# Transform tables as two 16-bit whole numbers per value, both parts written by ScalarE

## The chip, the cores and the metric

The kernel runs as one program on one core of a Trainium2 chip. The metric is the device time of one execution, in microseconds (us). The core has a matrix engine (TensorE, PE in the profile, with its weight loads as PEld), VectorE (DVE), ScalarE (ACT), GpSimd (POOL) and a queue engine that issues transfers (SyncE, SP).

## The reference

Three stages follow each other:

```python
X = np.fft.fft(x, axis=1); X = np.fft.fft(X, axis=2); x = X.real     # x: 8 x 3072 x 256
logits = x @ w_gate; e = argmax(logits); p = softmax(logits)[e]      # 8 experts, 768 tokens each at most
out[i] = p * (relu(x[i] @ w1[e]) @ w2[e])      # the first tokens of each expert only, 0 for the rest
h = out @ w_in; y = maximum(0.01 * h, h) @ w_out                     # 256 -> 2048 -> 256
```

Only the first 768 tokens of each expert are kept, in the order of the sequence. The kernel transforms just as many batches as it takes to fill the experts, and a branch at the end covers inputs for which these do not do.

## The kernel before, in words

All matrix work is done in pairs: a value is held as a high part and a low part (`split`, L190: ScalarE copies the value into a tile of the matrix format, which rounds it; VectorE subtracts that from the value), and a product takes three matmuls (`mm3`, L194, the matmuls of L199 to L201).

The transform along the sequence is a product with cosine and sine tables. `shape_consts` (L46) computes them on the host, 128 x 6918 values. `load_table` (L293) brings them in three parts j, each in two halves of 128 x 1153: a transfer into a staging tile `tst`, then one step that splits it into `th` and `tl`. SP's transfers run in the order of the code: the first block of x (`xj`), two halves of tables, the next block of x, two halves, the third block, two halves, then small constants.

Before the matmuls, `fold_steps` (L329) folds each block of x on VectorE: two large sums and differences (`fe`, `xj`), then smaller ones down to `raw`. Three blocks make a batch. `fsplit_j` (L409) splits `raw` into `fh` and `fl`. `s1_first` (L512) multiplies these by the tables for batch 0, block by block, into eight banks. `s1_ev_odd` and `s1_ev_even` (L454, L467) take them out to `pch`, `pcl`, `psh`, `psl`. `build_gate` (L251) makes the movable matrix of the second transform with the gate's columns, `smov` for one of the rows that need an own treatment, `special` (L581) the stationary side of these, `spec`. Then `s2_steps` (L622) runs the transform along the channels: its first matmul (L643, `psu<-smov,spec`) needs both. The first three batches (0, 1 and half of 2) go through this, with the folds of the next batch and the routing of the last (`route`, L709) strewn in between. Then the tokens are gathered and go through the experts (`moe_static`, L1257) and through the dense layers at the end.

On all engines but SP the order of instructions comes from a list scheduler, which works from its own estimates of durations when the program is built. A change of one step's cost or engine can therefore move other instructions.

Of the kernel before, what the change touches and what calls it, by code (L numbers as in the profile page):

```python
# [8 lines left out]
F32 = mybir.dt.float32  # L9
F32R = mybir.dt.float32r  # L10
BF16 = mybir.dt.bfloat16
I32 = mybir.dt.int32
ALU = mybir.AluOpType
ACTF = mybir.ActivationFunctionType
AX = mybir.AxisListType
# [5 lines left out]
P = 128  # L21
# [14 lines left out]
TJ = 2306  # L36
T_OFF = {"A": (0, 384), "B": (768, 384), "C": (1152, 386), "D": (1538, 384), "E": (1922, 384)}
T_W = 3 * TJ


def s_rows():

    return np.concatenate([np.arange(0, 384, 2), np.arange(1, 384, 2)]).reshape(3, P)


def shape_consts():  # L46
    w = 2 * np.pi / S
    n = np.arange(384)
    nc_ = np.arange(386)
    parts = []  # L50
    for s in s_rows().astype(np.float64):
        z = s == 0
        u2 = np.where(z, 384, 768 - s)
        s3 = np.where(z, 384, s)
        tc_ = np.cos(w * np.outer(s, 4 * nc_))
        tc_[:, 385] = 0.0
        te = np.sin(w * np.outer(s, 4 * n))
        te[z] = 0.0
        parts += [np.cos(w * np.outer(s, 4 * n + 1)), np.cos(w * np.outer(u2, 4 * n + 1)),
                  np.cos(w * np.outer(s, 4 * n + 2)), tc_, np.sin(w * np.outer(s3, 4 * n + 2)), te]  # L60
    c = {"tab": np.concatenate(parts, 1).astype(np.float32)}
    assert c["tab"].shape == (P, T_W)
    alt = np.zeros((1, 386), np.float32)
    alt[0, :385] = (-1.0) ** np.arange(385)
    c["altn"] = alt
    d = np.arange(P, dtype=np.float64)
    l = np.arange(D, dtype=np.float64)
    cd = np.cos(2 * np.pi / D * np.outer(d, l))
    sd = np.sin(2 * np.pi / D * np.outer(d, l))
    cd[0] = 1.0  # L70
    sd[0] = 0.0
    c["mcs"] = np.stack([cd, sd, -sd], 1).astype(np.float32)
    altl = (-1.0) ** l - 1.0
    lt = np.concatenate([cd.T.reshape(2, P, P), sd.T.reshape(2, P, P),
                         np.repeat(altl.reshape(2, P, 1), 96, axis=2)], 2)
    c["mcsT"] = np.ascontiguousarray(
        np.concatenate([lt[:, :, :256], lt[:, :, 256:]], 2).transpose(1, 0, 2)).astype(np.float32)

    def spec(nb):
        m = np.zeros((96, nb, D), np.float32)  # L80
        k = np.zeros((96, nb, 2), np.float32)
        for b in range(nb):
            for h in range(2):
                r = h * nb + b
                m[r, b] = altl
                m[32 + r, b] = altl
                k[r, b, 0] = k[32 + r, b, 0] = 1.0
                k[64 + r, b, 1] = 1.0
        return m, k

    c["sm3"], c["sk3"] = spec(NSTAT)
    c["sm1"], c["sk1"] = spec(1)
    p = np.arange(P)
    tri = np.stack([(p[:, None] < p[None]), (p[:, None] > p[None]), np.ones((P, P))], 1)
    c["tri"] = tri.astype(np.float32)
    rid = np.full((P, NCH), 1536.0 + 3 + P, np.float32)
    tok = np.full((P, NCH), 1536.0, np.float32)
    inval = np.zeros((P, NCH), np.float32)
    for i in range(3):
        for r in range(4):  # L100
            k = 4 * (128 * i + p) + r
            tok[:, 4 * i + r] = k
            rid[:, 4 * i + r] = P + k
            mcol = 13 + 4 * (2 - i) + 3 - r
            tok[:, mcol] = S - k
            rid[:, mcol] = P + 1536 + 4 * (128 * i + p) + 3 - r
    inval[1:, 12] = 100.0
    inval[0, 24] = 100.0
    inval[:, 25] = 100.0
    rt = np.stack([rid, tok], 1)  # L110
    c["rt"], c["inval"] = np.stack([rt + S * b for b in range(NSTAT)], 1).astype(np.float32), inval
    c["iota"] = np.tile(p, (P, 1)).astype(np.float32)
    c["w8"] = np.tile(8.0 - np.arange(8, dtype=np.float32), (P, 1))
    keep = np.ones((P, E, NG + 1), np.float32)
    keep[:, :, 0] = 0.0
    c["keep"] = keep
    return c
# [26 lines left out]
class Kern:  # L144
# [39 lines left out]
    def tt(self, o, x, y, op):  # L184
        self.nc.vector.tensor_tensor(out=o, in0=x, in1=y, op=op)  # L185
# [4 lines left out]
    def split(self, hi, lo, src):  # L190
        self.act(hi, src)
        self.tt(lo, src, hi, ALU.subtract)

# [57 lines left out]
    def build_gate(self, tmp, nb):  # L251
# [24 lines left out]
        for b in range(nb):  # L276
            t0 = tmp.tile([96, E], F32, name="smt0", tag="smt0")
            V.tensor_scalar(out=t0, in0=wh.bitcast(F32), scalar1=sk[:, b, 0:1], scalar2=None, op0=ALU.mult)
            t1 = tmp.tile([96, E], F32, name="smt1", tag="smt1")
            V.tensor_scalar(out=t1, in0=wl.bitcast(F32), scalar1=sk[:, b, 1:2], scalar2=None, op0=ALU.mult)  # L280
            self.tt(mv[:, b, D:], t0, t1, ALU.add)

# [6 lines left out]
    def open_tables(self):  # L289
        self.th = self.big.tile([P, T_W + 13 * 96], F32R, name="th", tag="bhi")  # L290
        self.tl = self.big.tile([P, T_W], F32R, name="tl", tag="blo")

    def load_table(self, pt, j):  # L293

        nc, a = self.nc, self.a
        st = []
        h = TJ // 2
        for i in range(2):
            t = pt.tile([P, h], F32, name="tst", tag=("pch", "pcl", "psh", "psl")[2 * (j % 2) + i])
            o = j * TJ + i * h  # L300
            nc.sync.dma_start(out=t, in_=a["tab"][:, o:o + h])
            st.append((1.3, lambda t=t, o=o: self.split(self.th[:, o:o + h], self.tl[:, o:o + h], t)))
        return st

    def tab(self, n, j, half=0):
# [23 lines left out]
    def fold_steps(self, b):  # L329
# [7 lines left out]
        tt = self.tt  # L337
        A, M = ALU.add, ALU.subtract

# [114 lines left out]
    def s1_ev_odd(self, fn, pa, pb):  # L454
# [5 lines left out]
        t3 = self.yp.tile([P, n], F32, name="t3", tag="ev", bufs=3)  # L460
        self.tt(t1, pa[:, :n], tb, ALU.add)
        x, y = (pa[:, :n], tb) if fn == "c" else (tb, pa[:, :n])
# [88 lines left out]
    def special_fold(self):  # L551
# [15 lines left out]
        tt(raw[0:1, 3, 0], ce[0:1, :, 0, 0], c7, A)  # L567
        st = self.th[:, T_W:].rearrange("p (k r) -> p k r", k=13)
        nc.gpsimd.memset(st.bitcast(F32), 0.0)
# [139 lines left out]
    def route(self, b, L, n):  # L709
# [9 lines left out]
        def t2(name, dt=F32):  # L719
            return rp.tile([P, NCH], dt, name=name, tag=name)[:, :n]  # L720
# [41 lines left out]
        def two():  # L762
# [31 lines left out]
            V.tensor_scalar(out=bad, in0=bad, scalar1=BIG, scalar2=float(E * self.capp), op0=ALU.mult, op1=ALU.add)  # L794
            ix = t2("rix", I32)
            self.tt(ix, sl, bad, ALU.add)
# [5 lines left out]
            else:  # L802
                hi, lo = (rp.tile([P, NCH], F32, name=f"slot{h}", tag=f"slot{h}", bufs=2)[:, :n] for h in "hl")
                for o, i, op, v in ((hi, "rih", ALU.logical_shift_right, 7), (lo, "ril", ALU.bitwise_and, 127)):
                    t = t2(i, I32)
                    V.tensor_scalar(out=t, in0=ix, scalar1=v, scalar2=None, op0=op)
# [162 lines left out]
    def prep(self, key, e, t, upto=None):  # L969
# [5 lines left out]
        else:  # L975
            rid = mx.tile([P, KT], F32, name="rid", tag="rid")
            nc.sync.dma_start(out=rid, in_=self.tbl[bass.ds(s0, T)].rearrange("(k p) c -> p (k c)", p=P))
        ix = mx.tile([P, KT, 2], I32, name="mix", tag="mix", bufs=self.live)
        no = mx.tile([P, KT], F32, name="no", tag="no", bufs=4)
# [453 lines left out]
    def build(self):  # L1433
        tc, nc = self.tc, self.nc
        self.fast = self.cap <= 2 * T
        with ExitStack() as es:
# [9 lines left out]
            with self.in_order("SP"):  # L1446
# [14 lines left out]
                flag = cst.tile([1, 2], F32, name="flag")  # L1461
                flag_i = cst.tile([1, 1], I32, name="flag_i")
                full = cst.tile([1, E], F32, name="full")
# [34 lines left out]
```

## Time and profile before

| | us |
|---|---|
| median of 3 runs | 1020.87 (1020.1 to 1021.87) |
| the profiled execution | 1019.98 |
| its span, from the first to the last instruction | 1018.1 |
| PE busy in the span | 952.1 (94%) |
| DVE busy | 636.4 (63%) |
| ACT busy | 480.9 (47%) |

The profile is of one execution. Times in its rows count from the start of the span. A busy share is a mean over all stages, so the table says which engine works most, and not what holds a given stage up; that is read from the rows of the stretch. A row of the timeline gives the start and the duration; the starts of two instructions that follow without a wait lie closer together than the duration, since an instruction begins before the one ahead has fully ended.

### The profile page before, as it was taken

The page shows a single profiled execution, that of the slowest core. Times are in us where ns is not written, and L with a number is a line of the kernel's source. Part 1 is how long each engine was busy: PE and PEld are TensorE (multiplying, and loading weights), DVE is VectorE, ACT ScalarE, POOL GpSimd, SP SyncE. Part 2 cuts the span into 40 slices and gives each one's busy share as a digit, 9 for nine tenths or more (in the row PEclk, how much of TensorE's full clock was granted, in tenths as well). Part 3 has the DMA queues.
Part 4 walks back from the last instruction along what each step waited for, and adds up shares of the span by engine and source line. Part 5 has one row for each costly group of instructions (what it writes and reads, how often), then busy time and mean ns, then how long its engine had stood idle before and what let it go on. Part 6 is the DMA issues. An engine that isn't in the chain of part 4 may idle for free. (4 is left out here: it accounts for less than half of the span.)

```text
span 1018.1 us, 15402 instructions
## 1 busy us (share of the span) xinstructions
PE 952.1 (94%) x5563; PEld 904.3 (89%) x5563; DVE 636.4 (63%) x1445; ACT 480.9 (47%) x1075; POOL 130.8 (13%) x178
## 2 busy tenths in 40 slices
PE   1749997999999999999999999999999999999996
PEld 1639996989999999998999999999999999999996
DVE  8997675879988544543555555555555555555553
ACT  4234631456665534443454444544444545454443
POOL 1000003065222121100011101110011001100111
PEclk9869997899999999999999999999999999999999
DMA  8324522379889666410010000000000000000000
GB/s 315 131 83 171 180 95 76 126 255 321 303 265 360 210 206 212 135 43 32 16 32 32 12 22 32 32 16 16 32 32 12 21 32 32 16 22 12 16 16 19
DMA packets 56193, 101.51 MB, mean 100 GB/s; under 512 B 5190, under 2 KB 39370, under 8 KB 54957
## 3 DMA queue, kind: packets, MB, share of 16 engines
q1 hardware_dynamic: 47000, 73.20, 21.5%
q0 software_dynamic: 4640, 12.81, 3.8%
q10 hardware_dynamic: 4468, 14.44, 3.5%
q8 instruction: 45, 0.74, 0.3%
q14 instruction: 40, 0.32, 0.1%
HBM read 54.54 MB, written 45.89 MB: 99 GB/s over the span
## 5 line engine op out<-in xcount | busy, mean ns | idle before, releaser
L185 DVE TENSOR_TENSOR gf<-gt,psg 128x384 f32<-128x384 f32 x256 | 141.7, 553 | 218.3 <-ACT gt L188 214.9
L188 ACT ACTIVATE gt<-psg 128x384 f32<-128x384 f32 x256 | 126.0, 492 | 253.7 <-PE psg L201 253.6
L1099 PE MATMUL po<-wo,gh 128*128 128x512 f32 x768 | 232.3, 394 | 0.0
L199 PE MATMUL psg<-yh,wi 128*128 128x384 f32 x512 | 172.7, 339 | 1.9 <-ACT yh L188 1.9
L200 PE MATMUL psg<-yl,wi 128*128 128x384 f32 x512 | 173.0, 338 | 0.0
L201 PE MATMUL psg<-yh,wi 128*128 128x384 f32 x512 | 172.6, 337 | 0.0
L185 DVE TENSOR_TENSOR gl<-gf,gh 128x384 fp32r<-128x384 f32 x256 | 141.3, 552 | 17.5 <-ACT gh L188 17.4
L1099 PEld LDWEIGHTS po<-wo,gh 128*128 128x128 f32 x768 | 139.7, 188 | 12.3
L1100 PE MATMUL po<-wo,gl 128*128 128x256 f32 x768 | 149.6, 281 | 0.0
L188 ACT ACTIVATE gh<-gf 128x384 fp32r<-128x384 f32 x256 | 132.8, 519 | 18.1 <-PE po L1099 17.8
L1100 PEld LDWEIGHTS po<-wo,gl 128*128 128x128 f32 x768 | 128.4, 188 | 4.0
L1110 POOL DMA_INDIRECT out<-ob,mix x48 | 47.0, 979 | 551.5 <-DVE ob L1109 475.8
L1042 DVE SCALAR_TENSOR_TENSOR hl<-psh,hh 128x384 fp32r<-128x384 f32 x128 | 69.9, 552 | 61.3 <-ACT hh L188 60.8
L199 PEld LDWEIGHTS psg<-yh,wi 128*128 128x128 f32 x512 | 96.7, 189 | 9.4 <-ACT yh L188 2.2
L200 PEld LDWEIGHTS psg<-yl,wi 128*128 128x128 f32 x512 | 96.7, 189 | 8.2
L201 PEld LDWEIGHTS psg<-yh,wi 128*128 128x128 f32 x512 | 96.5, 188 | 2.1
L199 PE MATMUL psh<-xTh,w1h 128*128 128x384 f32 x256 | 87.0, 342 | 2.3 <-DVE hl L1042 1.5
L199 PE MATMUL psy<-hh,w2h 128*128 128x384 f32 x256 | 87.9, 343 | 0.5 <-DVE hl L1042 0.3
L200 PE MATMUL psh<-xTl,w1h 128*128 128x384 f32 x256 | 86.4, 338 | 0.0
L201 PE MATMUL psh<-xTh,w1l 128*128 128x384 f32 x256 | 86.3, 337 | 0.0
L201 PE MATMUL psy<-hh,w2l 128*128 128x384 f32 x256 | 86.3, 337 | 0.0
L200 PE MATMUL psy<-hl,w2h 128*128 128x384 f32 x256 | 86.3, 337 | 0.0
(224 smaller groups left out, 1425.0 us busy)
## 6 DMA issues: line engine op xcount, KB each, us to landing
out<-zero SPq DMA_DIRECT2D x48, 512.0 KB
xj<-in_xg SPq DMA_DIRECT2D x9, 1024.0 KB
w1r<-in_w SPq DMA_DIRECT2D x9, 1024.0 KB
w2r<-in_w SPq DMA_DIRECT2D x9, 1024.0 KB
y_kept<-yf ACTq DMA_DIRECT2D x16, 384.0 KB
yf<-y_kept SPq DMA_DIRECT2D x16, 384.0 KB
y_first<-yd ACTq DMA_DIRECT2D x9, 530.0 KB
w<-in_w_in SPq DMA_DIRECT2D x8, 512.0 KB
```

The source lines that it names most:

```text
L185: self.nc.vector.tensor_tensor(out=o, in0=x, in1=y, op=op)
L188: self.nc.scalar.activation(out=o, in_=x, func=func, scale=scale)
L199: nc.tensor.matmul(out=out, lhsT=lh, rhs=rh, start=start and i == 0, stop=False)
L200: nc.tensor.matmul(out=out, lhsT=lh, rhs=rl, start=False, stop=False)
L201: nc.tensor.matmul(out=out, lhsT=ll, rhs=rh, start=False, stop=stop and i == n - 1)
L1042: nc.vector.scalar_tensor_tensor(out=lo, in0=ps[:, :T], scalar=0.0, in1=hi.bitcast(F32), op0=ALU.max, op1=ALU.subtract)
L1099: mm(out=o, lhsT=gh[:, c], rhs=both, start=f == 0, stop=False)
L1100: mm(out=o[:, :D], lhsT=gl[:, c], rhs=first, start=False, stop=f == NF2 - 1)
L1110: i = nc.gpsimd.indirect_dma_start(out=self.a["out"][0:nr], out_offset=bass.IndirectOffsetOnAxis(ap=s["ix"][:, k, 1:2], axis=0), in_=ob, i ...
```

## The change

The host gives each table value as two 16-bit whole numbers, a multiple of 2^-12 and a remainder as a multiple of 2^-27. The staging tile holds both, 2 x 1153 numbers of 2 bytes in place of 1153 of 4. ScalarE writes the high part and the low part, each with one activation that multiplies by a power of two. The subtraction on VectorE is gone. Each half of a part is still one transfer of 4612 bytes per partition, and the order on SP stays.

```diff
+TAB_HI, TAB_LO = 12, 27
...
+    hi = np.rint(tab * 2.0 ** TAB_HI)
+    lo = np.rint((tab - hi * 2.0 ** -TAB_HI) * 2.0 ** TAB_LO)
+    c = {"tab": np.stack([v.reshape(P, 6, TJ // 2) for v in (hi, lo)], 2).astype(np.int16)}
...
-            t = pt.tile([P, h], F32, name="tst", tag=("pch", "pcl", "psh", "psl")[2 * (j % 2) + i])
+            t = pt.tile([P, 2, h], I16, name="tst", tag=("pch", "pcl", "psh", "psl")[2 * (j % 2) + i])
             o = j * TJ + i * h
-            nc.sync.dma_start(out=t, in_=a["tab"][:, o:o + h])
-            st.append((1.3, lambda t=t, o=o: self.split(self.th[:, o:o + h], self.tl[:, o:o + h], t)))
+            nc.sync.dma_start(out=t, in_=a["tab"][:, 2 * j + i])
+            st.append((1.3, lambda t=t, o=o: (self.act(self.th[:, o:o + h], t[:, 0], scale=2.0 ** -TAB_HI),
+                                              self.act(self.tl[:, o:o + h], t[:, 1], scale=2.0 ** -TAB_LO))))
```

The change moves instructions at places of which the diff tells nothing. Line numbers of the changed kernel are higher by up to 6.

The first place is the start of ScalarE's program, where `th` and `tl` are the tables, `fh` the high part of a folded block and `xh` a row of its own. Before:

```order
L188 ACTIVATE okc<-tab 128x2
L188 ACTIVATE th<-tst 128x1153 x3
L188 ACTIVATE xh<-ee 1x128
L188 ACTIVATE th<-tst 128x1153
L188 ACTIVATE fh<-raw 128x8x128
L188 ACTIVATE th<-tst 128x1153 x2
L188 ACTIVATE yx<-rt 1x1
```

With the change:

```order
L193 ACTIVATE xh<-ee 1x128
L193 ACTIVATE th<-tst 128x1153
L193 ACTIVATE tl<-tst 128x1153
L193 ACTIVATE fh<-raw 128x8x128
L193 ACTIVATE th<-tst 128x1153
L193 ACTIVATE tl<-tst 128x1153
L193 ACTIVATE fh<-raw 128x8x128
L193 ACTIVATE th<-tst 128x1153
L193 ACTIVATE tl<-tst 128x1153
L193 ACTIVATE th<-tst 128x1153
L193 ACTIVATE tl<-tst 128x1153
L193 ACTIVATE yx<-rt 1x1
```

Ahead of `xh` stand four more such rows, for two halves. Each `th` is followed by its `tl`, and the second `fh` now comes ahead of the last four table passes.

The second place is VectorE where the first block of batch 0 is folded (`fe`, `xj`, `ce`, `raw`). Before:

```order
L185 TENSOR_TENSOR xj<-xj 128x4x128
L185 TENSOR_TENSOR tl<-tst,th 128x1153
L185 TENSOR_TENSOR ce<-fe 128x256
L185 TENSOR_TENSOR raw<-fe 128x2x128
L185 TENSOR_TENSOR se<-xj 128x256
L185 TENSOR_TENSOR raw<-xj 128x2x128
L185 TENSOR_TENSOR tl<-tst,th 128x1153
L185 TENSOR_TENSOR raw<-ce 128x128 x2
```

With the change:

```order
L190 TENSOR_TENSOR xj<-xj 128x4x128
L190 TENSOR_TENSOR ce<-fe 128x256
L190 TENSOR_TENSOR raw<-fe 128x2x128
L190 TENSOR_TENSOR se<-xj 128x256
L190 TENSOR_TENSOR raw<-xj 128x2x128
L190 TENSOR_TENSOR raw<-ce 128x128 x2
```

Both subtractions are gone here, and so are the four further on.

The third place is VectorE just ahead of `smov`, which the first matmul of the second transform waits for. `smt` are the two parts that `smov` adds; the `xj`, `ce`, `raw`, `se` around them fold the last block of batch 1, and `fe<-xj` begins batch 2. Before:

```order
L185 TENSOR_TENSOR tx<-ps_443,tb 96x384 x2
L185 TENSOR_TENSOR xj<-xj 128x4x128
L185 TENSOR_TENSOR ce<-fe 128x256
L185 TENSOR_TENSOR raw<-fe 128x2x128
L280 TENSOR_SCALAR smt_413<-wl,skf 96x8
L185 TENSOR_TENSOR spec<-tx,spec 32x384 x2
L185 TENSOR_TENSOR se<-xj 128x256
L185 TENSOR_TENSOR raw<-xj 128x2x128
L185 TENSOR_TENSOR raw<-ce 128x128 x2
L185 TENSOR_TENSOR fe<-xj 128x1024
L185 TENSOR_TENSOR smov<-smt_411,smt_413 96x8
L185 TENSOR_TENSOR fl<-raw,fh 128x768
```

With the change:

```order
L190 TENSOR_TENSOR ee<-xe 1x128
L190 TENSOR_TENSOR smov<-smt_411,smt_413 96x8
L190 TENSOR_TENSOR spec<-tx,spec 32x384
L190 TENSOR_TENSOR xj<-xj 128x4x128
L190 TENSOR_TENSOR ce<-fe 128x256
L190 TENSOR_TENSOR raw<-fe 128x2x128
L283 TENSOR_SCALAR smt_416<-wh,skf 96x8
L285 TENSOR_SCALAR smt_418<-wl,skf 96x8
L190 TENSOR_TENSOR se<-xj 128x256
L190 TENSOR_TENSOR raw<-xj 128x2x128
L190 TENSOR_TENSOR raw<-ce 128x128 x2
L190 TENSOR_TENSOR fe<-xj 128x1024
```

The rows from `xj<-xj 128x4x128` to `fe<-xj` of these blocks stood ahead of `smov` and now stand behind `smov` and the last `spec`. All other rows ahead of `smov`, the six `tl` apart, are the same in number and size.

## Rows read from the trace of the kernel before

**Rows 1.** The page's part 1: busy time, share of the span, instructions.

```profile
PE 952.1 (94%) x5563; PEld 904.3 (89%) x5563; DVE 636.4 (63%) x1445; ACT 480.9 (47%) x1075; POOL 130.8 (13%) x178
```

**Rows 2.** Busy time by stretch: length, engines with instruction counts, PEclk (granted clock), DMA share, GB/s.

```profile
7.38:38.22 30.84, 12.52 (x60) 10.95 (x60) 30.84 (x69) 11.44 (x19) 0.00 (x0) 0.94 0.66 236
...
5.93:67.78 61.85, 25.64 (x127) 21.91 (x127) 61.59 (x140) 23.42 (x44) 0.00 (x0) 0.84 0.51 182
67.78:160.00 92.22, 92.08 (x669) 88.52 (x669) 67.39 (x223) 41.24 (x125) 0.77 (x5) 0.98 0.38 139
160.00:176.00 16.00, 9.24 (x47) 7.27 (x46) 7.76 (x39) 1.30 (x4) 6.45 (x10) 0.62 0.21 68
176.00:216.00 40.00, 36.86 (x202) 35.82 (x203) 32.93 (x101) 18.84 (x42) 11.43 (x20) 0.90 0.49 163
...
480.00:1018.00 538.00, 529.50 (x3030) 495.69 (x3028) 291.60 (x567) 255.88 (x566) 46.98 (x48) 1.00 0.07 22
```

**Rows 3.** Waits of the first 100 us: total, times, longest.

```profile
PE ps L199 <- ACT fh L188: 26.8, 3, 20.7
PE psu L643 <- DVE smov L185: 15.1, 1, 15.1
```

**Rows 4.** Timeline of PE behind the wait: start, duration; idle before and its releaser.

```profile
67.92 0.56 PE L643 MATMUL psu<-smov,spec 96*128 96x264 f32 x1 [15.06 <-DVE smov L185]
```

**Rows 5.** The staging tile's instructions: duration in ns as minimum, median, maximum.

```profile
L188 ACT ACTIVATE th<-tst x6: 1147/1158/1166, 7.4 to 21.6; 128x1153 fp32r<-128x1153 f32 x6
L185 DVE TENSOR_TENSOR tl<-tst,th x6: 1341/1342/1352, 9.5 to 26.9; 128x1153 fp32r<-128x1153 f32 x6
```

**Rows 6.** Timeline of DVE, start of the program.

```profile
5.93 1.22 DVE L185 TENSOR_TENSOR fe<-xj 128x1024 f32<-128x1024 f32 x1 [2.62 <-DMA xj<-in_xg]
...
9.54 1.35 DVE L185 TENSOR_TENSOR tl<-tst,th 128x1153 fp32r<-128x1153 f32 x1
10.81 0.42 DVE L185 TENSOR_TENSOR ce<-fe 128x256 f32<-128x256 f32 x1
```

**Rows 7.** Timeline of DVE ahead of smov.

```profile
62.84 0.67 DVE L185 TENSOR_TENSOR xj<-xj 128x512 f32<-128x512 f32 x1
...
64.11 0.21 DVE L280 TENSOR_SCALAR smt<-wl,skf 96x8 f32<-96x8 f32 x1
...
65.40 0.43 DVE L185 TENSOR_TENSOR se<-xj 128x256 f32<-128x256 f32 x1
...
67.62 0.16 DVE L185 TENSOR_TENSOR smov<-smt,smt 96x8 fp32r<-96x8 f32 x1
```

**Rows 8.** Timeline of ACT: first table pass, two in a row, third fh, first eviction.

```profile
7.38 1.17 ACT L188 ACTIVATE th<-tst 128x1153 fp32r<-128x1153 f32 x1 [5.15 <-DMA tst<-in_tab]
...
12.66 1.16 ACT L188 ACTIVATE th<-tst 128x1153 fp32r<-128x1153 f32 x1 [2.72 <-DMA tst<-in_tab]
...
20.58 2.21 ACT L188 ACTIVATE th<-tst 128x1153 fp32r<-128x1153 f32 x2
...
38.22 1.06 ACT L188 ACTIVATE fh<-raw 128x1024 fp32r<-128x1024 f32 x1 [2.61 <-DVE raw L185]
...
43.62 0.49 ACT L188 ACTIVATE tb<-ps 128x384 f32<-128x384 f32 x1 [0.73 <-PE ps L201]
```

**Rows 9.** Timeline of SP: an issue pair of x blocks, the second held up.

```profile
23.96 12.45 SPq L326 DMA_DIRECT2D xj<-in_xg  x2
```

**Rows 10.** Timeline of DVE: first eviction, the fold of batch 1 begins, routing waits.

```profile
36.38 1.21 DVE L185 TENSOR_TENSOR fe<-xj 128x1024 f32<-128x1024 f32 x1
...
45.55 1.00 DVE L185 TENSOR_TENSOR t<-ps,tb 128x384 f32<-128x384 f32 x2
...
93.22 0.37 DVE L733 TENSOR_REDUCE mx<-L 128x26 f32<-128x208 f32 x1 [4.19 <-ACT L L188]
```

**Rows 11.** Timeline of ACT: reads of whole numbers and of floats, both small.

```profile
110.83 0.21 ACT L188 ACTIVATE sloth<-rih 128x26 f32<-128x26 int32 x1
...
114.61 0.23 ACT L188 ACTIVATE L<-yd 128x32 f32<-128x32 f32 x1
```

More of the change, by code (lines that the diff above doesn't have):

```diff
@@ L12 @@
 I32 = mybir.dt.int32
+I16 = mybir.dt.int16
 ALU = mybir.AluOpType
@@ L60, in shape_consts @@
                   np.cos(w * np.outer(s, 4 * n + 2)), tc_, np.sin(w * np.outer(s3, 4 * n + 2)), te]
-    c = {"tab": np.concatenate(parts, 1).astype(np.float32)}
-    assert c["tab"].shape == (P, T_W)
+    tab = np.concatenate(parts, 1)
+    assert tab.shape == (P, T_W)
+    hi = np.rint(tab * 2.0 ** TAB_HI)
+    lo = np.rint((tab - hi * 2.0 ** -TAB_HI) * 2.0 ** TAB_LO)
+    c = {"tab": np.stack([v.reshape(P, 6, TJ // 2) for v in (hi, lo)], 2).astype(np.int16)}
     alt = np.zeros((1, 386), np.float32)
```

## The prediction

> **What bounds the kernel now.** The page's first part is where one begins, and it points the wrong way: PE is busy for 94% of the span and DVE for 63% [rows 1]. These are means over stages. The table of stretches parts them [rows 2]. From 67.78 us to 160, PE is busy for 92.08 of 92.22 us, and from 480 to the end for 529.50 of 538: there the matmuls set the time. But from 5.93 to 67.78 PE works 25.64 of 61.85 us and DVE 61.59. In this first stretch VectorE is full from its first large fold [rows 6] to the last input of the second transform.
>
> The list of waits says what this costs: PE waits once for 15.1 us for `smov`, and 26.8 us in three waits for `fh` [rows 3]. The timeline shows the first of these end at 67.92, when `psu` starts [rows 4], 0.14 us after `smov` ends on DVE [rows 7]. So the start of the long PE stretch is set by the number of microseconds of work that VectorE has ahead of `smov`, and what goes from there goes from the total, as long as nothing else comes late.
>
> **What the change takes off VectorE.** Six subtractions of 128x1153, 1.342 us each [rows 5]. One begins at 9.54 and the row behind it at 10.81 [rows 6], so each takes 1.27 us of the engine's queue: 6 x 1.27 = 7.6 us. All six are issued by 26.9 [rows 5], thus all lie ahead of `smov`.
>
> **What moves.** The order of the changed program puts the rest of batch 1's last fold and the first step of batch 2 behind `smov` and `spec`; they stood ahead of it. By the starts before, the first group lasts from 62.84 to 64.11 (1.27) and the second from 65.40 to 67.62 (2.22) [rows 7]: 3.5 us more off the path. They are not saved, since DVE does them later, but then PE has matmuls of batch 0 to run meanwhile. Their users are the `fl` of batch 1 and its stage of matmuls. Before, DVE waits 4.19 us at 93.22 for the outputs of the second transform [rows 10]. With the moved block back in front, DVE reaches that place 7.6 us earlier and PE's output comes about 10.7 earlier, so some 1 us of the cushion is left and DVE is still not late.
>
> **What is added on ScalarE.** Six more passes over 128x1153. Two in a row take 2.21 us [rows 8], so 1.10 each: 6.6 us, in a stretch where ACT is busy for 23.42 of 61.85 us [rows 2]. Whether they lie on the path is decided at the third `fh`, which releases PE's last block of stage one. It starts at 38.22 after waiting 2.61 us for VectorE [rows 8]. DVE will deliver its input earlier by the 7.6 us and by about 2.6 of rows that have moved behind it, the largest being the `fe` of 36.38 [rows 10]: at 38.22 - 7.6 - 2.6 = 28.0. ScalarE must be free by then. It begins at 7.38 [rows 8], and from there to that `fh` it was busy for 11.44 us [rows 2]; with the added 6.6 that is 18.0. On top comes a wait for the third half of the tables, whose pass began at 12.66 when it had landed [rows 8]: four passes and a small row from 7.38 on end at about 12.1, so 0.6. ScalarE is done at 7.38 + 18.0 + 0.6 = 26.0. That leaves 2.0 us, so I cost the added passes at nothing; what hides them is ScalarE's idle time ahead of that `fh`.
>
> No row before has ScalarE read 16-bit whole numbers. The nearest: a read of 32-bit whole numbers, 26 wide, took 0.21 us and a read of 32-bit floats, 32 wide, 0.23 [rows 11]; so the type costs nothing there. Bounds: 1.0 us for a pass (a little below the 1.10, since a pass reads half the bytes) and 2.2 (half the rate). I take 1.10, by the read of whole numbers. The Trainium skill, "ScalarE: Activation LUTs", section "What ACT_TABLE_LOAD costs", gives 186 ns plus 0.833 per column for an activation with immediate scale, fp32 and bf16 alike; worked out for 1153 columns that is an estimate of 1147 ns. The shortest pass here is 1147 [rows 5], so they agree for floats, and the page says nothing of whole numbers of 16 bits.
>
> **What becomes late next.** Two places on VectorE. (1) The first eviction `t` needs ACT's `tb`, which came 5.4 us after the third `fh` began (43.62 - 38.22) [rows 8]: now 33.4. DVE reached `t` at 45.55 [rows 10]; with all that is taken off or moved behind it, 11.6 us by the row spacings, it is there at about 33.9. So this wait is about nil, at most 1 us. (2) Batch 1's first block of x. SP issued it at 23.96 [rows 9] and will not be later, since the buffer comes free sooner; 1 MiB at the stretch's mean of 182 GB/s [rows 2] takes 5.8 us, so it lands by 29.7. DVE wants it at 36.38 - 7.4 = 29.0 [rows 10], by the six subtractions less 0.2 for small rows that have moved. Again at most 1 us. I take 0.4 us for both, with 0 and 2 as ends. SP's order and bytes are as before, so the pair's second issue, which waits for a fold, comes with the folds.
>
> **The sum.** `psu` starts at 67.92 - 7.6 - 3.5 + 0.4 = 57.2, a gain of 10.7 us. From there PE is full to 160, so the shift is kept. Between 160 and 216 PE idles 6.76 + 3.14 = 9.9 us [rows 2], in a chain of routing, gathers and transposes that starts from PE's own outputs; it moves as a block. The scheduler's order differs a little there; I take 0, with a third of that idle time (3.3 us) either way as a bound. From 480 on, PE is busy for 98% again. The profiled execution took 1019.98 us, so it becomes 1009.3; the median of the runs is 0.89 above it, so 1020.87 - 10.7 = **1010.2 us**.
>
> **The rivals.** *A, forecast:* the gain is the removed work and the moved block, 9 to 13 us, 1008 to 1012. For it: one engine full to 0.26 us in 61.85 and PE waiting for it. Chance 0.60.
>
> *B, only the removed work counts, less the new waits:* the moved block's place is taken by waits for PE's evictions, for x, or by a worse order from 160 to 216. 1020.87 - 7.6 = 1013.3, and with the 2 us of late arrivals 1015.3. For it: two arrivals with under 1.5 us to spare. Against it: both lie far ahead of `smov`. Chance 0.22. A better order from 160 to 216 on top of A (10.7 + 3.3 = 14.0, 1006.9 or less) has 0.07.
>
> *C, no change:* PE is the engine of this kernel, and work off VectorE is hidden. It would need the wait of 15.1 us for `smov` to be filled by something else as long, such as `special` on PE and ScalarE, which ends before it. The time would be 1020.9. Against it speaks the stretch from 5.93 to 67.78 [rows 2]. Chance 0.07. The Trainium skill, "Perfetto Trace Analysis", section "Identifying the Most-Contended Engine", has it this way: the engine of the highest occupancy (for TensorE its weight loads' busy share) is to be worked on. By that rule it is TensorE, at 89% against 63% [rows 1], and 1020.9 would be its result; the trace agrees with it only if it is asked stretch by stretch.
>
> *D, slower:* ScalarE's read of 16-bit numbers runs at a lower rate, and the third `fh` stands behind twelve such passes. ScalarE has 2.0 us to spare, so the point where it begins to set the time is 1.10 + 2.0/12 = 1.27 us a pass, and the gain is gone at 1.10 + (2.0 + 10.7)/12 = 2.16. At a third of the rate, 3.3 us, the passes add 26.4, less 2.0 and 10.7: 13.7 us slower, 1034.6. For it: no such read in the trace, and the second half begins 2306 bytes into the tile. Against it: the rate for 32-bit whole numbers [rows 11]. Chance 0.04.
>
> **How the numbers follow.** A difference of 0.2% is 2.04 us, about what a measurement of this kernel can tell from none. A, B and the better order are faster: 0.89. C is the same: 0.07. D is slower: 0.04. The range of 8 in 10 holds A and B and leaves out most of the rest: its lower end is 1020.87 - 14.0, rounded down to 1006.5, and the upper 1015.3 rounded up to 1016.
>
> **What would show it.** In the changed profile: no `tl` on DVE and twelve table passes on ACT of 1.1 to 1.2 us each; the third `fh` near 28; `psu` starting near 57, with PE's wait for `smov` still some 15 us, since all ahead of it moves together; DVE still full up to there; then PE full to about 149, and all later stages earlier by the same amount. I am wrong if the passes take 1.3 us or more, if DVE shows idle time of over 2 us ahead of `smov`, or if the gain at `psu` shrinks between 149 and 205.

## The result, and the profile after

| | before | after |
|---|---|---|
| median of 4 runs each, same chip (us) | 1021.13 | 1011.46 |
| lowest and highest | 1020.1 to 1021.87 | 1010.51 to 1011.9 |
| the profiled execution | 1019.98 | 1011.39 |
| its span | 1018.1 | 1009.6 |
| start of `psu` in it | 67.92 | 56.26 |

The ratio is 0.9911, with a 95% interval of 0.9897 to 0.9926: faster, by 9.7 us in the medians. The prediction was 1010.2 us, in a range from 1006.5 to 1016. The time is inside the range and 1.3 us above the forecast. Of that, 0.3 us is in the median of before, which is 1021.13 beside these runs and was 1020.87 beside the ones shown earlier. The gain itself is known to about 1 us: the ratio makes it 9.1 us, and two later sets of runs of the same kernel gave 8.5 and 8.8. The rest of the miss comes from two terms of the sum that missed in opposite directions. They are followed below.

The page's part 1 of the kernel after: busy time, share of the span, instructions.

```profile
PE 952.0 (94%) x5563; PEld 903.9 (90%) x5563; DVE 628.6 (62%) x1439; ACT 487.0 (48%) x1081; POOL 127.1 (13%) x178
```

Against [rows 1], DVE has six instructions less and 7.8 us less work, ACT six more and 6.1 us more, and PE's work is the same. The kernel is faster although its busiest engine does exactly what it did.

The staging tile's instructions after: duration in ns as minimum, median, maximum, then first and last start.

```profile
L193 ACT ACTIVATE th<-tst x6: 1147/1150/1166, 7.4 to 22.8; 128x1153 fp32r<-128x1153 int16 x6
L193 ACT ACTIVATE tl<-tst x6: 1147/1150/1157, 8.4 to 23.8; 128x1153 fp32r<-128x1153 int16 x6
```

These answer to [rows 5]. No `tl` is left on VectorE, and a pass over 16-bit whole numbers takes 1150 ns, where one over floats took 1158.

Timelines of the kernel after, one engine after the other: ACT's third `fh`; VectorE around `smov`; PE's start of the second transform; VectorE's routing.

```profile
28.05 1.06 ACT L193 ACTIVATE fh<-raw 128x1024 fp32r<-128x1024 f32 x1 [1.39 <-DVE raw L190]
```

```profile
29.04 1.20 DVE L190 TENSOR_TENSOR fe<-xj 128x1024 f32<-128x1024 f32 x1
...
34.04 1.00 DVE L190 TENSOR_TENSOR t<-ps,tb 128x384 f32<-128x384 f32 x2
...
55.96 0.15 DVE L190 TENSOR_TENSOR smov<-smt,smt 96x8 fp32r<-96x8 f32 x1
56.14 0.55 DVE L190 TENSOR_TENSOR spec<-tx,spec 32x384 fp32r<-32x384 f32 x1
56.72 0.69 DVE L190 TENSOR_TENSOR xj<-xj 128x512 f32<-128x512 f32 x1
...
80.66 0.35 DVE L739 TENSOR_REDUCE mx<-L 128x26 f32<-128x208 f32 x1
```

```profile
56.26 0.56 PE L649 MATMUL psu<-smov,spec 96*128 96x264 f32 x1 [15.39 <-DVE smov L190]
```

The third `fh` starts at 28.05 (28.0 was predicted) and it is still VectorE that it waits for, so the added passes are hidden. The two arrivals that were to be late, `fe` at 29.04 and `t` at 34.04, show no wait at all. PE still waits 15.4 us for `smov`, as in [rows 3]: everything ahead of it has moved as a block. `psu` starts 11.66 us earlier than in [rows 4]. The moved fold stands behind `smov`, and when VectorE comes to `mx` at 80.66, the outputs are there.

Busy time by stretch after; the columns are those of [rows 2].

```profile
5.90:56.20 50.30, 23.86 (x127) 20.39 (x127) 50.05 (x125) 26.72 (x47) 0.00 (x0) 0.90 0.60 221
...
56.26:148.61 92.35, 92.35 (x671) 88.68 (x672) 70.62 (x232) 43.58 (x128) 0.77 (x5) 0.98 0.38 140
148.61:164.17 15.56, 8.86 (x44) 7.03 (x43) 7.68 (x39) 1.22 (x4) 6.32 (x10) 0.59 0.21 70
```

VectorE is again full up to `smov` (50.05 of 50.30 us), and PE from there to 148.61 without a gap. The whole difference is that the first stretch is shorter.

Where it is kept, and where not, is seen by landmarks. The gathered tokens go through the experts in 16 tiles of 384, and each tile opens with transposes of its gathered rows `xg` (`pst<-ident,xg`). The starts of these are good marks on PE's timeline. Worked out from them, in us:

```
                                  before   after   shift
start of psu                       67.92   56.26  -11.66
tile 2, first transpose           186.77  174.96  -11.81
tile 5, first transpose           248.46  238.01  -10.45
tile 8, first transpose           302.23  292.66   -9.57
last pass of ScalarE (ob)        1009.31 1000.03   -9.28
```

The shift is whole up to tile 2. Between tile 2 and tile 8 it loses 2.2 us, and then it nearly stays. The last 0.8 us of the span (8.5 of gain there) lie behind the last `ob`; in three profiles of the kernel after that tail is 9.6, 9.0 and 8.8 us long, so this is scatter of single executions.

Two more profiles of the kernel after (`after_again`, `after_third`) show what repeats. Their tile 2 comes 10.12 and 10.81 us earlier than before, so the table's 11.81 is the best of the three; from tile 2 to tile 8 they lose 2.65 and 2.66 us.

### The profile page after: what moved, and what is told of

The parts are those of the page before. It is cut to its first block, busy times and chain, and to the rows that moved or that the text cites. A ratio compares the mean times of both kernels' runs of the same rounds, so it can differ in the third digit from the quotient of the medians.

```text
span 1009.6 us, 15401 instructions
## 1 busy us (share of the span) xinstructions
PE 952.0 (94%) x5563; PEld 903.9 (90%) x5563; DVE 628.6 (62%) x1439; ACT 487.0 (48%) x1081; POOL 127.1 (13%) x178
## 5 line engine op out<-in xcount | busy, mean ns | idle before, releaser
L193 ACT ACTIVATE hh<-psh 128x384 fp32r<-128x384 f32 x128 | 62.4, 492 | 50.4 <-PE psh L206 46.6
```

Of the source, the lines that this page charges most:

```text
L193: self.nc.scalar.activation(out=o, in_=x, func=func, scale=scale)
```

## The experiments

Two questions: does the time hang on VectorE's work ahead of `psu` alone, and what took back 2.2 us between tiles 2 and 8?

**The subtraction twice.** The kernel before, with one more of the removed instruction per half table:

```diff
-            ... self.split(self.th[:, o:o + h], self.tl[:, o:o + h], t)))
+            ... (self.split(self.th[:, o:o + h], self.tl[:, o:o + h], t),
+                 self.tt(self.tl[:, o:o + h], t, self.th[:, o:o + h], ALU.subtract))))
```

> The kernel before, with each of the six table subtractions on VectorE done twice, so six more of 1.27 us of its queue, all ahead of smov; nothing is left out. Theory A (the second transform starts when VectorE has worked through what stands ahead of smov): psu starts at 67.9 + 7.6 = 75.5 us and the whole takes 7 to 9 us more, about 1028.5. Rival C (VectorE's work is hidden under TensorE's): psu stays at 68 and the time at 1021. A rise of about half would mean that only part of VectorE's queue is on the path.

Measured: 1027.74 us beside 1020.49 of before, ratio 1.0075 (1.0058 to 1.0091). PE's start of the second transform:

```profile
75.60 0.56 PE L643 MATMUL psu<-smov,spec 96*128 96x264 f32 x1 [11.96 <-DVE smov L185]
```

`psu` is 7.68 us later, six times 1.28, and the time 7.25 longer. This work is on the path at full price, and rival C (no change) is out.

**ScalarE's low pass twice.** The kernel after, `tl` written two times, 18 passes in place of 12:

```diff
-   self.act(self.tl[:, o:o + h], t[:, 1], scale=2.0 ** -TAB_LO)
+   self.act(self.tl[:, o:o + h], t[:, 1], scale=2.0 ** -TAB_LO), self.act(self.tl[:, o:o + h], t[:, 1], scale=2.0 ** -TAB_LO)
```

> The changed kernel, with each of the six low parts written twice by ScalarE, so 18 table passes and not 12; nothing is left out. In this build the scheduler leaves the last fold block of batch 1 ahead of smov, as in the kernel before. Theory A: what counts is VectorE's queue, so the gain at psu is the 7.6 us of subtractions without the 3.5 of the moved block: psu at 60.3, plus up to 1.5 us since the third fh now waits for ScalarE (its idle time of 1.4 us ahead of that fh is less than the 6.3 added). Time 1013 to 1015. Rival D' (ScalarE's cover is used up, and each further pass costs its full 1.05 us): psu at 60.3 + 5 = 65.3, time near 1018.

Measured: 1012.3 us, ratio to before 0.993 (0.9914 to 0.9947). The expectation had 1013 to 1015, 0.7 us too high. The third `fh`, `smov` and `psu` of this kernel:

```profile
30.17 1.04 ACT L193 ACTIVATE fh<-raw 128x1024 fp32r<-128x1024 f32 x1
```

```profile
60.46 0.16 DVE L190 TENSOR_TENSOR smov<-smt,smt 96x8 fp32r<-96x8 f32 x1
```

```profile
60.77 0.56 PE L649 MATMUL psu<-smov,spec 96*128 96x264 f32 x1 [15.94 <-DVE smov L190]
```

Here the third `fh` no longer waits for VectorE: it follows a `tl` pass without idle time. So six more passes of 1.05 us (6.3) have used up the margin, and `fh` is 2.1 us later than after. `psu` is 4.5 us later than after, but that is mostly another thing: with the added work the scheduler leaves batch 1's last fold ahead of `smov`, as in the kernel before (`xj` of 128x512 at 55.68, `fe` of 128x1024 at 59.33). VectorE's rows ahead of `smov` are here exactly those of before without the six subtractions. Against before, `psu` gains 7.15 us, the six subtractions less 0.45. Thus the six passes of the change are hidden, six more are not quite, and what moves behind `smov` in the change is worth some 4 us of its own (4.5 less the 0.45). The time gains more than `psu` does, 8.2 us; 1.3 of it lies behind tile 8, where this execution has no fall of the clock at the dense layers (705.78 us to the last `ob`, 707.08 before; see below).

**The low part on VectorE, from the 16-bit numbers.** The kernel after, with this one operation moved back:

```diff
-   self.act(self.tl[:, o:o + h], t[:, 1], scale=2.0 ** -TAB_LO)
+   self.nc.vector.tensor_scalar(out=self.tl[:, o:o + h], in0=t[:, 1], scalar1=2.0 ** -TAB_LO, scalar2=None, op0=ALU.mult)
```

> The changed kernel with the low part written by VectorE from the 16-bit numbers, one multiplication with a constant per half and no subtraction; the high part stays on ScalarE. VectorE's order is that of the kernel before row for row. Theory A: the gain is 6 times the difference between 1.27 us and the new pass. If the pass takes 0.8 us (by the 128x512 rows with one source, 0.34 us from start to start), psu is at 65.1 and the time 1018; if it takes 1.27, all gain is gone, 1021. Rival (the gain comes from the table being free of the high part, so that both parts can be written without waiting for each other, not from VectorE's queue): psu at 57 to 60, time 1011 to 1014.

Measured: 1017.14 us, ratio 0.9972 (0.996 to 0.9985). The staging tile's instruction on VectorE:

```profile
L308 DVE TENSOR_SCALAR tl<-tst x6: 741/744/755, 9.0 to 24.1; 128x1153 fp32r<-128x1153 int16 x6
```

```profile
64.06 0.15 DVE L190 TENSOR_TENSOR smov<-smt,smt 96x8 fp32r<-96x8 f32 x1
```

```profile
64.37 0.56 PE L649 MATMUL psu<-smov,spec 96*128 96x264 f32 x1 [13.57 <-ACT fh L193]
```

Ahead of `smov` VectorE has the rows of before, with this pass in place of the subtraction; the order is not that of before row for row, as was expected, since some early rows have changed places. The profile puts PE's wait down to an `fh`, but `psu` starts 0.16 us after `smov` ends, as in the other kernels. It is 3.55 us earlier than before. By the durations six passes save 6 x (1.342 - 0.744) = 3.6 us. So without the moved block the gain is just the difference of the work, and the 16-bit format with the work left on VectorE is worth a third of the whole.

**Batch 1's folds all behind `smov`.** If 3.5 us of fold behind `smov` pay, perhaps more do. The kernel after with VectorE held to the order of the code up to `special`, and the waiting folds released behind it:

```diff
+        fio = ExitStack()
+        fio.enter_context(self.in_order("DVE"))
         run(fs[0], fs[1], fs[3], *tb[0])
...
         run(ev[0], ev[1], lambda: self.build_gate(self.tmp, NSTAT), ev[2], ev[3], self.special)
+        self.upto()
+        fio.close()
```

> The changed kernel with VectorE held to the order of the code from the start to the end of batch 1's fold, so that this fold (some 16 us that now lies ahead of smov) comes behind spec and smov. Theory A: psu starts when VectorE and the evictions are through, near 45 us, and TensorE's wait of 15.4 us ahead of psu is mostly gone. Then batch 1's fold and its fl end about when TensorE comes to that batch (45 + 24 = 69), so a new wait of 1 to 4 us there; time 1000 to 1005. Rival (something else, such as ScalarE or TensorE's own chain, holds psu near 56): time 1010 to 1012. Rival 2: the gain of 11 us at psu is wholly given back by the wait for batch 1's fold: time 1010 as well, but with psu near 45 and a wait of some 10 us near 69.

Measured: 1030.08 us, ratio 1.0097 (1.008 to 1.0114). Slower than before, and the expectation was wrong. VectorE's waits on its way to `smov` and to the last `spec`; the start of `psu`; a later stretch with the columns of [rows 2], and PE's wait in it:

```profile
39.19 1.02 DVE L190 TENSOR_TENSOR t<-ps,tb 128x384 f32<-128x384 f32 x2 [3.92 <-ACT tb L193]
...
45.61 0.17 DVE L190 TENSOR_TENSOR mvcl<-ps_c,mvch 128x8 fp32r<-128x8 f32 x1 [2.59 <-ACT mvch L193]
...
46.99 0.17 DVE L190 TENSOR_TENSOR smov<-smt,smt 96x8 fp32r<-96x8 f32 x1
...
50.89 1.03 DVE L190 TENSOR_TENSOR psl<-t,psh 128x384 fp32r<-128x384 f32 x2 [1.62 <-ACT psh L193]
```

```profile
57.34 0.56 PE L649 MATMUL psu<-smov,spec 96*128 96x264 f32 x1 [7.42 <-DVE spec L190]
```

```profile
100.00:120.00 20.00, 11.24 (x51) 10.29 (x52) 18.87 (x62) 3.82 (x7) 0.38 (x1) 0.61 0.01 4
```

```profile
109.85 0.19 PE L761 MATMUL psr<-rs,tri 128*128 128x32 bf16 x1 [8.54 <-DVE rs L754]
```

`smov` is there at 46.99, 9 us earlier than in the kernel after, but in this order `psu` waits for `spec`, and starts at 57.34, later than in the kernel after: without the folds between, VectorE comes too early to what PE and ScalarE deliver. The folds then stand in VectorE's queue later. From 100 to 120 us VectorE works 18.87 of 20, PE waits 8.54 us for `rs`, a step of the routing, and works 11.24 of 20, where it was full before [rows 2]. So the fold is cover for waits as well as a burden. The run changes two things at once, the place of the folds and the order of all else in the front, which is now that of the code; a finer order was not tried.

**The gate's steps later.** What is lost between tiles 2 and 8? With each gathered row come its 8 logits, and the step `gate` of each tile begins with a reduction of them on VectorE, `gm<-xg` (L1005), which needs all rows of the tile. In the kernel after, for the third tile:

```profile
198.60 0.53 DVE L1048 SCALAR_TENSOR_TENSOR hl<-psh,hh 128x384 fp32r<-128x384 f32 x1
201.56 0.18 DVE L1005 TENSOR_REDUCE gm<-xg 128x3 f32<-128x24 f32 x1 [2.43 <-DMA xg<-y_first,mix]
201.65 0.68 DVE L190 TENSOR_TENSOR w2l<-w2r,w2h 128x512 fp32r<-128x512 f32 x1
202.25 0.69 DVE L190 TENSOR_TENSOR wi<-r,lf 128x512 fp32r<-128x512 f32 x1
202.85 0.56 DVE L1048 SCALAR_TENSOR_TENSOR hl<-psh,hh 128x384 fp32r<-128x384 f32 x1
```

VectorE waits 2.43 us for the gathered rows with `w2l`, `wi` and `hl` queued behind. In the kernel before, these stood ahead of it:

```profile
211.56 0.68 DVE L185 TENSOR_TENSOR wi<-r,lf 128x512 fp32r<-128x512 f32 x1
212.16 0.55 DVE L1042 SCALAR_TENSOR_TENSOR hl<-psh,hh 128x384 fp32r<-128x384 f32 x1
213.43 0.18 DVE L999 TENSOR_REDUCE gm<-xg 128x3 f32<-128x24 f32 x1 [0.71 <-issue]
```

TensorE's order differs too. The transposes of this tile after, and before:

```profile
199.85 0.62 PE L1029 MATMUL pst<-ident,xg 128*128 128x128 f32 x2 [1.16 <-DMA xg<-y_first,mix]
201.52 0.66 PE L1029 MATMUL pst<-ident,xg 128*128 128x128 f32 x4 [1.05 <-DMA xg<-y_first,mix]
```

```profile
211.92 0.69 PE L1023 MATMUL pst<-ident,xg 128*128 128x128 f32 x4 [1.30 <-DMA xg<-y_first,mix]
215.76 0.39 PE L1023 MATMUL pst<-ident,xg 128*128 128x128 f32 x2
```

After, the six stand in one row of the program and wait twice for gathered rows; before, four and two, with 3 us of matmuls between, and PE waits once. Neither difference is in the diff; the list scheduler has come to another order. The gate has three steps in the code: `gate` (maximum and difference, VectorE), `gate1` (exponential, ScalarE) and `gate2` (sum and reciprocal, VectorE). The test moves the first two of them two places later and the third one place, in the kernel after and, as a control, in the kernel before, beside the kernel after itself:

```diff
-        if f == 3:
+        if f == 5:
             self.gate(key)
-        if f == 6:
+        if f == 7:
             self.gate2(key)
...
-        if f == 4:
+        if f == 6:
             self.gate1(key)
```

> The changed kernel with the gate's three small steps of each expert tile (mask product, reduce, reciprocal) placed two steps later in the code; the front up to psu keeps its order. Theory (2.3 us of the 11.7 gained at psu are given back at the second gather because the scheduler's order there puts six transposes of the third tile in a row and the gate's reduce ahead of work that PE needs): here the transposes stand as 2 and 4 with matmuls between, so psu stays at 56.3, the shift of 11.7 against before is kept to within 1 us behind that place, time 1009.0 to 1010.4. Rival (the gathered rows or the weights come from memory when they come, and any order waits for them): the shift shrinks to 9.3 to 9.6 again, time 1011 to 1012.

> The same move of the gate's steps in the kernel before, as a control. Theory: before loses nothing at that place, so psu stays at 67.9 and the time within 0.8 us of before, 1020 to 1021.5. If it is faster by 2 us or more, the move is a gain of its own and says nothing of what the change lost.

> The changed kernel with line breaks alone altered. Both theories: psu at 56.3, the same order at the second gather, six transposes in a row with waits of about 1 us for the gathered rows, the shift down from 11.7 to about 9.3 behind it, time 1011 to 1012. If those waits are gone in this execution, what was lost there is chance and not the order.

Measured beside 1019.85 us of before: the kernel after 1011.35 us, ratio 0.9911 (0.9896 to 0.9927); with the gate later 1008.29, ratio 0.9884 (0.9868 to 0.9899); the control 1019.83, ratio 0.9999 (0.999 to 1.0008). The later gate is worth nothing before and 3.1 us after. In the kernel with the gate later:

```profile
200.10 0.68 DVE L190 TENSOR_TENSOR wi<-r,lf 128x512 fp32r<-128x512 f32 x1
200.70 0.55 DVE L1048 SCALAR_TENSOR_TENSOR hl<-psh,hh 128x384 fp32r<-128x384 f32 x1
...
202.18 0.18 DVE L1005 TENSOR_REDUCE gm<-xg 128x3 f32<-128x24 f32 x1 [0.86 <-DMA xg<-y_first,mix]
```

`gm<-xg` stands behind `wi` and `hl` again, as before, and the transposes stand as two and four. What was expected of the time (1009.0 to 1010.4) was still 0.7 us too high.

**Other places for the gate.** The same three lines with other numbers: one step earlier (2, 3, 5), two earlier (1, 2, 4), one later (4, 5, 7). Of the names in the expectations, `sq` and `lf` are steps that turn the dense layers' weights into pairs, and `oha`, `ohr` the two sides of the products that make the token table.

> The changed kernel with the gate's steps one step earlier in the code. TensorE's order is the changed kernel's own, six transposes of the third tile in a row; on VectorE sq and lf still stand ahead of the last four pairs oha, ohr, as in the changed kernel. Theory (that order at the second gather costs some 1.5 to 2.5 us): no better than the changed kernel, 1010.8 to 1012.3. Rival (what counts is the gate's own place, late is good): no better either, perhaps worse. Rival (executions differ by chance, the clock, and no order is better): 1009.5 to 1012.

> The gate's steps two steps earlier in the code. Here the order comes out with oha, ohr ahead of sq and lf and the third tile's transposes as 2 and 4, as when they are two steps later. Theory of the order: as fast as with the gate two steps later, 1007.8 to 1010. Rival (the gate's own place): 1011 or more. Rival (chance): 1009.5 to 1012.

> The gate's steps one step later. The order has oha, ohr ahead of sq and lf and the transposes as 2, 2 and 2. Theory of the order: 1007.8 to 1010. Rival (the gate's own place): between the changed kernel and the one with the gate two steps later, 1009.5 to 1010.5. Rival (chance): 1009.5 to 1012.

Measured beside 1020.46: one earlier 1010.52 (ratio 0.9901, 0.9886 to 0.9916), two earlier 1013.54 (0.9931, 0.9918 to 0.9945), one later 1008.86 (0.9894, 0.9875 to 0.9912). The first is 0.3 us below its expected range, inside that of the rival by chance; the third came as the order's theory had it. The second is a miss: it has the transposes as two and four and `gm<-xg` behind `wi`, and is the slowest. So the number of transposes in a row is no measure of how good the order is.

**Once more, side by side.** The kernel with the gate two steps later, and the kernel after:

> The changed kernel with the gate's steps two steps later, a second time. Theory (the gate's reduce on VectorE, behind wi and hl in place of ahead of them, spares TensorE 2 to 3 us at the second gather): 2 to 3.5 us below the changed kernel in the same set of runs, 1007.5 to 1009.3. Rival (the first comparison was chance of the clock): within 1 us of it.

> The changed kernel itself beside it. Both: 1010.5 to 1012; from the second group of transposes to the fifth 63.0 to 63.5 us, as in both of its profiles so far, by the theory; down to 61 by the rival.

Measured beside 1020.21: 1008.07 us (ratio 0.9891, 0.9873 to 0.9908) and 1011.46 (0.9913, 0.99 to 0.9926). The difference is there again, 3.4 us. The ratios' intervals still touch at their ends, as they did in the first set (0.9899 and 0.9896), since single executions of the kernel with the gate later scatter from 1006.39 to 1012.1. Twice 3 us between medians, with the control at nothing, is what speaks for it.

Stretches from tile 2 to tile 5, columns as in [rows 2]: before; after; the third profile of after; the gate one step earlier; two steps later, twice; one step later; two steps earlier.

```profile
186.77:248.46 61.69, 57.57 (x332) 55.88 (x330) 55.05 (x142) 34.73 (x75) 27.76 (x42) 0.97 0.77 257
```

```profile
174.96:238.01 63.05, 58.98 (x332) 57.47 (x331) 54.35 (x140) 35.21 (x75) 25.42 (x42) 0.95 0.74 251
```

```profile
175.96:239.39 63.43, 58.02 (x332) 55.85 (x331) 54.38 (x140) 34.78 (x75) 24.90 (x42) 0.97 0.74 250
```

```profile
176.40:239.59 63.19, 58.02 (x331) 55.89 (x330) 54.15 (x140) 34.95 (x75) 24.90 (x42) 0.97 0.74 251
```

```profile
176.49:237.08 60.59, 55.96 (x332) 54.22 (x331) 53.73 (x141) 34.52 (x75) 24.05 (x42) 1.00 0.77 257
```

```profile
175.00:236.06 61.06, 57.34 (x332) 55.94 (x330) 54.59 (x142) 34.74 (x75) 23.63 (x42) 0.97 0.77 259
```

```profile
175.56:236.07 60.51, 55.97 (x332) 54.30 (x331) 53.75 (x140) 34.57 (x75) 27.16 (x42) 1.00 0.77 257
```

```profile
176.00:240.03 64.03, 57.93 (x332) 55.96 (x330) 54.79 (x143) 34.70 (x75) 29.36 (x42) 0.97 0.74 247
```

The length is the first number behind the start and the end. With `gm<-xg` ahead of `wi` and `hl` it is 63.05 to 63.43 (all three profiles of after, and the gate one step earlier); behind them 60.51 to 61.69, in before too, but for the last.

The other kernels divide in the same way. Counted from tile 2 to tile 8, where the whole loss lies, the four profiles with `gm<-xg` ahead and that of the folds behind `smov`, which has it ahead too, take 117.05 to 118.12 us. Those with it behind take 114.80 to 115.63: before, its control, the gate one and two steps later, and also the subtraction twice, ScalarE's pass twice and the low part on VectorE. The last two are the changed kernel with the gate where it was; there the scheduler came to the old order by itself and nothing was lost. The exception is the gate two steps earlier, with 117.44. In it PE waits once more behind the second gather:

```profile
211.34 0.44 PE L204 MATMUL psh<-xTh,w1h 128*128 128x384 f32 x1 [1.03 <-DVE xTl L190]
```

and POOL waits 20.2 us for the token table `tab`, where in after it waits 18.6. It seems a different loss by the same kind of cause, which no run tests. So the place of `gm<-xg` goes with the loss in thirteen profiles of fourteen, but each kernel differs in the order of a whole stretch: that this row alone makes the loss is not shown. PE's own wait for the gathered rows at that place does not go with it: 2.21 us in the kernel after, 2.72 and 1.28 in the two profiles with the gate two steps later.

Within the stretch the loss has two parts that differ from one execution to the next: idle time of PE (4.1 us in the first profile of after, as in before, and 5.4 in the third) and work at a lower clock (PE busy 58.98 and 58.02 us, 57.57 before; 55.96 where the clock was full throughout). The sum repeats to 0.4 us, the parts do not, so I don't put one number to the waits alone.

The version with the gate two steps later beats both kernels: in its two sets of runs it is 11.6 and 12.1 us faster than before, 3.1 and 3.4 than after. Some of that is not the second gather: in its two profiles the part from tile 8 to the last `ob` takes 705.85 and 706.09 us, in the three of after 707.35 to 707.43, and 707.08 before. There TensorE waits 1.88 us for `yh` as the dense layers begin, and its granted clock falls behind this wait in the kernel after (0.52 from 462 to 464 us) and in before (0.50 from 471.5 to 473.5), but stays at 1.00 in that version, with the same wait. Why is open; so up to 1.5 of the 3.1 and 3.4 us may be no merit of the order.

## Why the prediction was right, and where its sizes were off

*What bounds.* That VectorE's work ahead of `smov` sets the end was right. In five kernels the time follows the start of `psu` nearly one for one. Each against before: 7.68 later gives +7.25 (subtraction twice), 3.55 earlier -3.35 (low part on VectorE), 7.15 earlier -8.2 (ScalarE's pass twice), 11.2 and 11.6 earlier -11.6 and -12.1 (gate two steps later, in its two sets), 11.3 earlier -11.6 (gate one step later). Others fall short, and the loss then lies behind `psu`: the kernel after, -9.7 for 11.66 (-8.5 and -8.8 for 11.5 and 11.4 in the later sets), and the gate one and two steps earlier, -9.9 and -6.9 for 11.4 and 11.3. With the folds behind `smov`, `psu` is 10.6 earlier and the time 9.6 longer. So the start of `psu` sets the end only as long as the order behind it holds.

The Trainium skill ("Perfetto Trace Analysis", section "Identifying the Most-Contended Engine") would have the engine of the highest occupancy worked on first, with TensorE judged by its weight loads' busy share. Over the whole span that is TensorE here, at 89% before and 90% after, and the 9.7 us came from an engine at 63%. The runs bear the rule out only where it is read by stretch: ahead of `psu` the fullest engine is VectorE, 61.59 of 61.85 us.

*The removed work.* 6 x 1.27 = 7.6 us, right: shown from both sides, by doubling it and by taking about half of it away.

*The moved block.* Put at 3.5 us. With the block ahead of `smov` the gain at `psu` is 7.15 (ScalarE's pass twice), with it behind 11.66. The 0.56 us that 7.6 and 3.5 do not explain is one more row that has moved: the last `spec` (0.55 us) now starts at 56.14, behind `smov`. The prediction counted only the rows from `xj` to `fe`, and it was said ahead of it that all other rows ahead of `smov` stay the same; in the two traces they do, but for this one. Not isolated by a run of its own.

*The added passes.* Costed at nothing, right. The margin was put at 2.0 us at the third `fh`, with ScalarE done at 26.0; in the changed profile it is done at 26.66 and idles 1.39 us right before that `fh`. Six passes more used it up. The price of a pass, taken as 1.10 from the read of floats, is 1.05 (`th` at 9.49, `tl` at 10.54): half of 2.21 us for two passes in a row counts a part of their overlap. The Trainium skill ("ScalarE: Activation LUTs", section "What ACT_TABLE_LOAD costs") gave an estimate of 1147 ns for 1153 columns of floats; the trace shows the same shortest pass, 1147 ns, for 16-bit whole numbers, of which that page is silent. Rival D is gone with that.

*Late arrivals.* Put at 0.4 us, with 2 as an end: nil. Batch 1's block was in time, as was `tb`. With this and the `spec`, `psu` gained 1.0 us more than predicted (11.66 for 10.7).

*The step that failed: "the scheduler's order differs a little there; I take 0".* Between tile 2 and tile 8 (186.77 to 302.23 before) the shift shrinks by 2.2 us, inside the bound of 3.3 that stood beside it, but not nil; part of it lies behind 216, where I had not looked for any. What the runs showed in its place: between tiles 2 and 5 the new order holds VectorE at `gm<-xg` ahead of `wi` and `hl`, and the stretch is longer (by 1.4 us in the first profile and 1.7 in the two others). Where that step stands behind them it is no longer than before, the gate two steps earlier excepted; that it is this row that does it, and not another of the same order, stays open. Between tiles 5 and 8 the fifth tile's transposes stand as three and three with waits for `hl` (0.31 and 0.52 us) and cost 0.9 us; the other two tiles of that part take what they took before, to 0.02 us. So 10.7 + 1.0 - 2.2 leaves 9.5; the medians say 9.7. That these agree to 0.2 is partly luck: the two profiled executions differ by 8.6 us, and the later sets by 8.5 and 8.8.

The last sign of being wrong, a gain at `psu` that shrinks between 149 and 205, named the right kind of loss. It came a little later: at tile 3 (199.85, before 211.92) the shift is still 12.07, at tile 4 (220.23, before 230.82) it is 10.59.

## What to carry to other kernels

Read which engine is full in the stretch ahead of a long wait, not over the span: six instructions off an engine at 63% were worth their whole length, because all of them stood ahead of one matmul, and an idle engine took over the work for nothing. When a scheduler orders the instructions, a shorter front can give another order far behind it, which here went with the loss of a fifth of the gain: compare landmarks along the whole trace, and where the shift shrinks look for a waiting instruction that has been put ahead of ready ones. Work that looks like ballast ahead of the critical step may be what fills the waits there; pushing all of it back, with the front in the order of the code, cost some 19 us (ratios of 1.0097 and 0.9911 to before) against the order that mixes them.

## What the hardware showed that was not expected

ScalarE reads 16-bit whole numbers with a scale at the rate of floats: 1150 ns for 128x1153 against 1158, also from a start in the middle of the tile. VectorE makes the same pass from one 16-bit source in 744 ns; the subtraction of two float sources took 1342.

After the same wait TensorE's full clock comes back at different times, in executions with the same instructions. Windows of 2 us from the start of `psu`, columns as in [rows 2], in two profiles of the kernel after:

```profile
56.20:58.20 2.00, 1.94 (x9) 1.98 (x10) 1.97 (x6) 0.08 (x1) 0.00 (x0) 0.50 0.00 0
58.20:60.20 2.00, 2.00 (x14) 2.00 (x14) 2.00 (x7) 1.91 (x5) 0.00 (x0) 0.73 0.24 37
60.20:62.20 2.00, 2.00 (x18) 2.00 (x18) 2.00 (x6) 2.00 (x6) 0.00 (x0) 1.00 0.84 295
```

```profile
56.40:58.40 2.00, 2.00 (x9) 2.00 (x10) 1.97 (x6) 0.14 (x1) 0.00 (x0) 0.50 0.00 0
58.40:60.40 2.00, 2.00 (x11) 2.00 (x11) 2.00 (x6) 1.91 (x5) 0.00 (x0) 0.50 0.23 37
60.40:62.40 2.00, 2.00 (x13) 2.00 (x12) 2.00 (x6) 2.00 (x6) 0.00 (x0) 0.63 0.83 307
```

The granted clock (third column from the right) is 0.50 at first, the level of 1.2 GHz, after 15.4 us in which PE stood, in both. In the first profile it is full (2.4 GHz) by 60.2, in the second by 62.4. From `psu` to 36 products in a row for the token table (148.61 and 149.86), with PE full all the way, the first took 92.35 us and the second 93.46; to tile 2, behind a second long wait, 118.70 and 120.25. A wait thus costs more than its length, and by an amount that differs by 1.1 us between these two executions; differences of that size between two profiles say nothing of the kernels.
